# Fewer weight chunks ahead of the first unit, decoded one unit later, and GpSimd's adds in reverse order

## The chip, the cores and the metric

The kernel runs on one core of one Trainium2 chip. The metric is the device time of one execution in microseconds (us); the time before the change is the median of three runs, 1470.31 us. Engines are called as in the profile: PE is TensorE's matmul and PEld its weight load, DVE is VectorE, ACT is ScalarE, POOL is GpSimd, SP is SyncE. ACTq and SPq are the sequencers that issue DMAs for ScalarE and SyncE.

## The reference

Attention with a top-32 mask, then a feed-forward block with the gate h * cos(h), on 8 batches of 8 heads, 576 positions, 64 values a head:

```
scores = q @ k.T / sqrt(64)                      # per batch and head
kth    = 32nd largest score of each row
attn   = softmax(where(scores >= kth, scores, -1e9))
x      = concat over heads (attn @ v)            # 4608 x 512
h      = x @ w_in                                # w_in: 512 x 2048
out    = (h * cos(h)) @ w_out                    # w_out: 2048 x 512
```

q, k and v are float32. The two weight matrices are float64: the kernel reads the two 32-bit words of every value and decodes them to float32 itself.

## The kernel before, in words

**Units and slots.** The work is cut into units: 128 tokens times one pair of heads (NP = 4 pairs), 144 units in all. A loop of slots runs over them. In slot i, VectorE searches the 32 largest scores of unit i in four rounds (L361 MAX8 and L366 MATCH_REPLACE8), on two folded halves of each row: `rest` holds the larger ones (made by VectorE, L256) and `low` the smaller ones (made by GpSimd, L274 and L283; in units 7 to 10 by VectorE, L264). In the same slot ScalarE masks and exponentiates the scores of unit i-1 (L390, L392, L400) and copies the scores of unit i+1 out of PSUM (L241, L244); GpSimd splits the exponentials of unit i-2 into 16-bit halves (L433, L435), which SyncE writes to DRAM (L443) and reads back transposed (L449); TensorE computes scores of later units (L229) and, every other slot, the values of two older units (L486), which VectorE takes over into `xT` (L495).

**Feed-forward.** As soon as the four units of a block of 128 tokens are done, TensorE also does the feed-forward matmuls of that block (L546 with w_in, L621 with w_out); ScalarE takes the first ones out of PSUM (L560, L562) and computes the sine (L601), GpSimd reduces and gates (L582, L591, L608).

**Weights.** The weights come in 32 chunks of 512 KB, 16 of w_in (numbers 0 to 15) and 16 of w_out. Each chunk goes through four steps, each with its own queue in `wq`:

- `load_weights`: the DMA into a staging tile `st` (L123). There are 7 tiles of tag "g", which the feed-forward shares later, and 4 of tag "x", which odd chunks below number 12 take.
- `decode_first`: two ScalarE operations (L136, L139) on the two words.
- `decode_second`: a shift on VectorE (L147, TENSOR_SCALAR).
- `decode_third`: an add on GpSimd (L157, TENSOR_TENSOR), after which the chunk is done.

In a slot, `load_weights` stands at the start, `decode_second` and `decode_third` between the third and the fourth round of the search, and `decode_first` at the end. So a chunk loaded in slot i is shifted and added in slot i+1. Ahead of slot 0 the kernel loads chunks 0 and 1 over SyncE's queue and six more over ScalarE's, and runs `decode_first` on four of them.

**What sets the order.** The order of instructions on each engine is the order of the program: an engine works its queue from front to back, and the DMAs that ScalarE issues stand in the same queue as its computing instructions. TensorE's feed-forward work is drawn slot by slot by a credit, and only from chunks that were done when the slot began:

```
wq["ready"] = wq["done"]
```

DMAs signal completion on eight semaphores, shared by both queues. A DMA is issued only when the DMA that had the same semaphore before it has landed.

Of the kernel before, what the change touches and what calls it, by code (L numbers as in the profile page):

```python
# [30 lines left out]
def kernel(  # L31
# [16 lines left out]
    NP = H // 2  # L48
# [37 lines left out]
    for i in range(DF // CW):  # L86
        w = consts.tile([P, NC, CW], F32, tag=f"w_in{i}", name=f"w_in{i}")
# [4 lines left out]
    for f in range(NF):  # L92
        w = consts.tile([P, DM], F32, tag=f"w_out{f}", name=f"w_out{f}")
# [6 lines left out]
    wq = {"next": 0, "loaded": deque(), "second": deque(), "third": deque(), "done": 0, "ready": 0}  # L100

    def staged(spare=0):
        return sum(c[2] == spare for k in ("loaded", "second", "third") for c in wq[k])

    def load_weights(n, queue=None):
        queue = queue or nc.scalar
        for _ in range(n):
            i = wq["next"]
            if i >= len(chunks):
                return  # L110
            src, dst = chunks[i]
            if not DECODE:
                queue.dma_start(out=dst, in_=src)
                wq["next"] = wq["done"] = i + 1
                continue
            spare = i < 3 * XB and i % 2 == 1 and staged(1) < XB
            if spare:
                st = ffw.tile([P, CW, 2], I32, tag="x", name="st", bufs=XB)
            elif staged() + ff["live"] >= CHUNKS:
                return  # L120
            else:
                st = ffw.tile([P, CW, 2], I32, tag="g", name="st", bufs=CHUNKS)
            queue.dma_start(out=st.rearrange("p w i -> p (w i)"), in_=src)  # L123
            wq["loaded"].append((st, dst, int(spare)))
            wq["next"] = i + 1
# [4 lines left out]
    def decode_first(n):  # L130


        for _ in range(min(n, len(wq["loaded"]))):
            st, w, spare = wq["loaded"].popleft()
            lo, hi = st[:, :, 0], st[:, :, 1]
            nc.scalar.activation(  # L136
                out=w, in_=hi.bitcast(F32), func=AF.Prelu, scale=2.0**-111, alpha=2.0**32
            )
            nc.scalar.mul(out=lo, in_=lo.bitcast(U32), mul=2.0**-29)  # L139
            wq["second"].append((st, w, spare))  # L140

    def decode_second(n):

        for _ in range(min(n, len(wq["second"]))):
            st, w, spare = wq["second"].popleft()
            wi = w.bitcast(I32)
            nc.vector.tensor_scalar(  # L147
                out=wi, in0=wi, scalar1=3, scalar2=None, op0=ALU.logical_shift_left
            )
            wq["third"].append((st, w, spare))  # L150

    def decode_third():

        while wq["third"]:
            st, w, _ = wq["third"].popleft()
            wi = w.bitcast(I32)
            nc.gpsimd.tensor_tensor(out=wi, in0=wi, in1=st[:, :, 0], op=ALU.add)  # L157
            wq["done"] += 1
# [63 lines left out]
    def scores(u):  # L222
        sc = u["sc"] = ps.tile([P, 2, 512], F32, tag="sc", name="sc", bufs=2)
        for to, k0, k1 in ((sc, 0, SB), (sc_ends[u["n"] % 2], SB, S)):
            for b, q0, rows, r0 in u["parts"]:
                for j in range(2):
                    d = slice(j * D, (j + 1) * D)
                    st = pairs[b, u["hp"]]
                    nc.tensor.matmul(  # L229
                        to[r0 : r0 + rows, j, 0 : k1 - k0],  # L230
                        st["q"][d, q0 : q0 + rows],
                        st["k"][d, k0:k1],
                        start=True,
                        stop=True,
                    )
# [42 lines left out]
    def fold_low(u):  # L278

        if not u["folds"] or u["n"] in BUSY:  # L280
            return
        low = u["low"].bitcast(I32)
        nc.gpsimd.tensor_tensor(  # L283
            out=low, in0=low, in1=u["rest"][:, :, HS:S].bitcast(I32), op=ALU.subtract
        )
# [15 lines left out]
    def topk_first(u, w):  # L301

        u["top"] = tops[u["n"] % len(tops)]
        merges = w and w["folds"]
        if merges:
            merge_first(w)
        if u["folds"]:
            if u["n"] not in BUSY:
                fold_sum(u)
            fold_high(u)  # L310
        else:
            u["rest"] = work.tile([P, 2, S], F32, tag="rest", name="rest", bufs=1)
        if merges:
            merge_second(w)
        if u["folds"] and u["n"] in BUSY:
            fold_now(u)
        topk_round(u, 0, [lambda: bounds(w), lambda: distances(w)] if w else ())

    def topk_round(u, rnd, between=(), ahead=None):
        top, rest, lasts = u["top"], u["rest"], TOPK // 8 - 1  # L320
        end = TOPK - 1 - 8 * rnd
        at = top[:, :, end : end - 8 if rnd < lasts else None : -1, 0]
        if u["folds"]:
            search(
                at, rest[:, :, HS:S] if rnd == 0 else rest[:, :, 0:HS], rest[:, :, 0:HS], rnd < lasts,
                between if rnd < lasts else (),
            )
        else:
            search(at, u["s"] if rnd == 0 else rest, rest, rnd < lasts, between)
        if rnd < lasts:  # L330
            return
        del u["rest"]
        if u["folds"]:
            low = u.pop("low")
            for k in range(TOPK // 16):
                more = k < TOPK // 16 - 1
                if ahead and not more:
                    take_values(ahead)
                search(
                    top[:, :, 1 + 8 * k : 9 + 8 * k, 1], low, low, more,  # L340
                    () if more or rnd < lasts else between,
                )
# [225 lines left out]
    def take_banks():  # L568
        while full:
            take, *what = full.popleft()  # L570
            take(*what)
# [83 lines left out]
    def feed(n):  # L655

        ff["tick"] += 1
        while n > 0 and ff["credit"] >= 1:
            for kind in (ff["kind"], 1 - ff["kind"]):
                if (can_first, can_second)[kind]():  # L660
                    break
            else:
                return
            if kind == 0:
                ff1(*first.popleft())
            else:
                ff2(*second.popleft())
            if kind != ff["kind"] or ff["half"]:
                ff["kind"], ff["half"] = 1 - kind, 0
            else:  # L670
                ff["half"] = 1
            n, ff["credit"] = n - 1, ff["credit"] - 1
# [24 lines left out]
    for n in range(NP, len(order)):  # L697
        i = last[order[n - 5]] if n >= 5 else 0
        load_at(max(i, 2 * NP + 2), load_qk, *order[n])
        i = last_values[order[n - 6]] if n >= 6 else 0  # L700
# [13 lines left out]
    def send(x):  # L714

        split(x)
        write_halves(x)
        transposes(x)

    def slot(i, u, w, x, z):  # L720
        n = 0 if i == 0 else 4 if i == 1 else 3 if i < NP else 2
        if i < NP:
            for load, b, hp in at_once[i]:
                load(b, hp)
        load_weights(n)
        if x:
            send(x)
        topk_first(u, w)
        fold_low(u)
        topk_round(u, 1)  # L730
        topk_round(u, 2)
        decode_second(NP)
        decode_third()
        made = scored.get(i, [])
        if z:
            take_banks()
        feed(1)

        for m in made:
            scores(m)  # L740
        if z:
            values(z)


        late = len(made) > 0

        decoding = i < 3 * NP
        if i % 2 or decoding:
            sines(1)
        if w:  # L750
            mask(w)
        take_banks()
        if w and late:
            exponentials(w)
        take_scores(units[i + 1])
        if w and not late:
            exponentials(w)
        topk_round(u, 3, both(w), z)
        if i in at_slot:
            load, b, hp = at_slot[i]  # L760
            load(b, hp)
        gate(1)
        feed(1 if len(made) == 2 else 2)
        take_banks()
        decode_first(NP)
        reduce_first()
        reduce_second()
        feed(1 if len(made) == 2 else 3)
        if i == LAST:
            sines(1)  # L770
# [46 lines left out]
    load_weights(2, nc.sync)  # L817
    scores(units[0])
    take_scores(units[0])
    load_weights(2 * NP - 2)  # L820
    decode_first(NP)
    for i in range(NU + 1):
        ff["end"] = i >= NU
        ff["credit"] = min(ff["credit"] + 5.0 - 0.9 * len(scored.get(i, [])), 5.3)
# [2 lines left out]
        u, w = (units[i - n] if 0 <= i - n < NU else None for n in range(2))  # L827
# [53 lines left out]
```

## Time and profile before

| | us |
|---|---|
| runs | 1470.68, 1468.21, 1470.31; median 1470.31 |
| profiled execution, its own time | 1467.61 |
| its span, first to last instruction | 1465.8 |
| busy PE | 1387.1 (95%) |
| busy DVE | 1363.0 (93%) |
| busy POOL | 1162.2 (79%) |
| busy ACT | 1086.8 (74%) |
| granted TensorE clock, mean | 0.972 |

The span is that of the profiled execution; 1.8 us of its own time lie outside it. A row of the timeline reads: start, duration, engine, line of the kernel, operation, output<-input, shape, count, and in brackets the idle time before it and what ended that wait. "x4" with one duration means four instructions in a row, from the first one's start to the last one's end. Times are from the start of the span.

### The profile page before, as it was taken

The page shows a single profiled execution, that of the slowest core. Times are in us where ns is not written, and L with a number is a line of the kernel's source. Part 1 is how long each engine was busy: PE and PEld are TensorE (multiplying, and loading weights), DVE is VectorE, ACT ScalarE, POOL GpSimd, SP SyncE. Part 2 cuts the span into 40 slices and gives each one's busy share as a digit, 9 for nine tenths or more (in the row PEclk, how much of TensorE's full clock was granted, in tenths as well). Part 3 has the DMA queues.
Part 4 walks back from the last instruction along what each step waited for, and adds up shares of the span by engine and source line. Part 5 has one row for each costly group of instructions (what it writes and reads, how often), then busy time and mean ns, then how long its engine had stood idle before and what let it go on. Part 6 is the DMA issues. An engine that isn't in the chain of part 4 may idle for free.

```text
span 1465.8 us, 30264 instructions
## 1 busy us (share of the span) xinstructions
PE 1387.1 (95%) x10290; PEld 996.1 (68%) x10290; DVE 1363.0 (93%) x5213; ACT 1086.8 (74%) x1911; POOL 1162.2 (79%) x814
## 2 busy tenths in 40 slices
PE   3378899999999999999999999999999999999998
PEld 2165667777777767777777767777777777777765
DVE  5999999999999999999999999999999999999831
ACT  5677777777777777777777777777777787777651
POOL 4978888888888887888888888888888888888510
PEclk6589999999999999999999999999999999999999
DMA  8777686666665566657665666656666466755200
GB/s 264 241 227 189 179 197 176 158 159 182 179 167 152 147 189 182 167 143 186 189 166 146 152 171 187 176 147 172 190 166 162 138 172 175 168 151 143 70 8 15
DMA packets 427433, 239.99 MB, mean 164 GB/s; under 512 B 375952, under 2 KB 392592, under 8 KB 427280
## 3 DMA queue, kind: packets, MB, share of 16 engines
q1 hardware_dynamic: 417552, 212.69, 55.2%
q10 hardware_dynamic: 9728, 25.38, 5.0%
q8 instruction: 81, 1.33, 0.4%
q14 instruction: 72, 0.59, 0.1%
HBM read 45.09 MB, written 101.19 MB: 100 GB/s over the span
## 4 chain that ended last, share of the span: by engine, by line
PE 81%; DVE 13%; ACT 4%; DMA 2%; issue 0%; POOL 0%; SPq 0%; ACTq 0%; POOLq 0%
PE mm L546 31%; PE o L621 31%; PE rim L486 10%; PE sc L229 7%; DVE top L361 6%; DVE rest L366 3%; PE rim L229 2%; DVE rest L256 1%; DVE low L366 1%; ACT s L400 1%; DMA st<-in_moe_w_in_dram 1%; DMA k<-in_k_dram 1%; DVE w_in L147 1%; ACT s L392 1%; ACT L400 1%
## 5 line engine op out<-in xcount | busy, mean ns | idle before, releaser
L546 PEld LDWEIGHTS mm<-xT,w_in 128*128 128x128 f32 x4608 | 536.6, 192 | 70.6 <-issue 64.1
L621 PE MATMUL o<-w_out,g 128*128 128x512 f32 x1152 | 538.9, 601 | 9.9 <-POOL g L608 8.7
L546 PE MATMUL mm<-xT,w_in 128*128 128x128 f32 x4608 | 539.9, 275 | 3.9 <-ACT x L562 2.0
L361 DVE MAX8 top<-rest 128x8 f32<-128x288 f32 x1148 | 480.6, 453 | 0.0
L433 POOL COPY halves<-s 128x2304 uint16<-128x2304 uint16 x140 | 294.4, 2103 | 151.2 <-ACT s L400 149.6
L366 DVE MATCH_REPLACE8 rest<-top,rest 128x288 f32<-128x288 f32 (+1 forms) x860 | 376.8, 445 | 0.0
L621 PEld LDWEIGHTS o<-w_out,g 128*128 128x128 f32 x1152 | 203.4, 191 | 199.4 <-issue 187.1
L361 DVE MAX8 top<-low 128x8 f32<-128x288 f32 x568 | 239.7, 447 | 0.0
L400 ACT ACTIVATE s<-s,nd 128x576 f32<-128x576 f32 x288 | 220.1, 767 | 1.2 <-ACT ob L631 0.4
L392 ACT ACTIVATE s<-s,top 128x576 f32<-128x576 f32 x288 | 206.2, 766 | 0.0
L283 POOL TENSOR_TENSOR low<-low,rest 128x576 int32<-128x576 int32 x138 | 194.8, 1411 | 10.8
L274 POOL TENSOR_TENSOR low<-s 128x576 int32<-128x576 int32 x138 | 194.6, 1410 | 6.9 <-ACT s L246 4.8
L229 PE MATMUL sc<-k,q 64*128 64x448 f32 (+1 forms) x640 | 157.2, 591 | 42.4 <-DVE rest L256 24.4
L560 ACT ACTIVATE g<-mm 128x512 f32<-128x512 f32 x144 | 85.8, 596 | 130.2 <-PE mm L546 126.0
L591 POOL TENSOR_TENSOR x<-g,x 128x1024 f32<-128x1024 f32 x68 | 160.8, 2365 | 5.7
L608 POOL TENSOR_TENSOR g<-g,x 128x1024 f32<-128x1024 f32 x68 | 160.8, 2364 | 1.6 <-ACT x L601 1.6
L486 PE MATMUL rim<-pT,v 128*64 128x128 f32 (+1 forms) x2560 | 159.0, 268 | 0.0
L486 PEld LDWEIGHTS rim<-pT,v 128*64 128x64 f32 x2560 | 132.5, 139 | 10.0 <-issue 2.0
L241 ACT COPY s<-sc 128x896 f32<-128x896 f32 x143 | 128.2, 897 | 0.5 <-PE sc L229 0.5
L366 DVE MATCH_REPLACE8 low<-top,low 128x288 f32<-128x288 f32 x284 | 123.5, 442 | 0.0
L244 ACT COPY s<-rim 128x256 f32<-128x256 f32 x144 | 55.0, 382 | 90.6 <-PE rim L486 90.6
L229 PEld LDWEIGHTS sc<-k,q 64*128 64x128 f32 (+1 forms) x640 | 46.7, 182 | 105.5 <-DVE rest L366 47.2
(62 smaller groups left out, 1336.4 us busy)
## 6 DMA issues: line engine op xcount, KB each, us to landing
rows<-halves SPq DMA_DIRECT2D x140, 640.0 KB, 3.0
out_dram<-ob ACTq DMA_DIRECT2D x36, 256.0 KB, 2.2
q<-in_q_dram SPq DMA_DIRECT2D x31, 288.0 KB, 3.8
v<-in_v_dram SPq DMA_DIRECT2D x32, 256.0 KB, 3.2
st<-in_moe_w_out_dram ACTq DMA_DIRECT2D x16, 512.0 KB, 5.4
st<-in_moe_w_in_dram ACTq DMA_DIRECT2D x14, 512.0 KB, 6.0
k<-in_k_dram SPq DMA_DIRECT2D x31, 144.0 KB, 3.7
k<-in_k_dram SPq DMA_DIRECT2D x32, 128.0 KB, 3.7
```

The costliest lines, as they stand in the source:

```text
L229: nc.tensor.matmul(to[r0 : r0 + rows, j, 0 : k1 - k0], st["q"][d, q0 : q0 + rows], st["k"][d, k0:k1], start=True, stop=True,)
L274: nc.gpsimd.tensor_tensor(out=u["low"].bitcast(I32), in0=s[:, :, 0:HS], in1=s[:, :, HS:S], op=ALU.add)
L283: nc.gpsimd.tensor_tensor(out=low, in0=low, in1=u["rest"][:, :, HS:S].bitcast(I32), op=ALU.subtract)
L361: nc.vector.max(to[:, j], src[:, j])
L366: nc.vector.match_replace(rest[:, j], to[:, j], src[:, j], NEG)
L392: nc.scalar.activation(out=s[:, j], in_=s[:, j], func=AF.Prelu, bias=less[:, j, 1:2], scale=1.0, alpha=FAR)
L400: nc.scalar.activation(out=s[:, j], in_=s[:, j], func=AF.Exp, bias=nd[:, j : j + 1], scale=SCALE, accum_out=den[:, j, 0:1],)
L433: nc.gpsimd.tensor_copy(out=halves[:, :, 0 : 2 * S], in_=s.rearrange("p (k h) -> p h k", h=2))
L486: nc.tensor.matmul(o[d, to], lhsT, rhs, start=c == 0, stop=c == NT)
L546: nc.tensor.matmul(mm[:, at : at + w], w_in[f // FC][:, c, (f % FC) * P : (f % FC + 1) * P], blk["xT"][:, c], start=c == 0, stop=c == NC - 1,)
L591: nc.gpsimd.tensor_tensor(out=x, in0=g, in1=x, op=ALU.subtract)
L621: nc.tensor.matmul(o, g[:, at : at + P], w_out[f], start=f == 0, stop=f == NF - 1)
```

## The change

Three edits. In the prologue, two weight chunks are issued on ScalarE's queue in place of six, and no `decode_first` runs there; the first chunks are decoded at the end of slot 0 and are shifted and added in slot 1. In `slot`, three chunks are loaded in slots 2 to 7 instead of in slots 2 and 3 only. In `decode_third`, the chunks of a slot are added from the last shifted one to the first.

```
     def decode_third():
 
         while wq["third"]:
-            st, w, _ = wq["third"].popleft()
+            st, w, _ = wq["third"].pop()
...
     def slot(i, u, w, x, z):
-        n = 0 if i == 0 else 4 if i == 1 else 3 if i < NP else 2
+        n = 0 if i == 0 else 4 if i == 1 else 3 if i < 2 * NP else 2
...
     load_weights(2, nc.sync)
     scores(units[0])
     take_scores(units[0])
-    load_weights(2 * NP - 2)
-    decode_first(NP)
+    load_weights(2)
```

The number of chunks that are shifted and added in each slot:

| slot | 0 | 1 | 2 | 3 | 4 | 5 | 6 | 7 | 8 | 9 | 10 | 11 |
|---|---|---|---|---|---|---|---|---|---|---|---|---|
| before | 4 | 4 | 4 | 3 | 3 | 2 | 2 | 2 | 2 | 2 | 2 | 2 |
| after | 0 | 4 | 4 | 3 | 3 | 3 | 3 | 3 | 3 | 2 | 2 | 2 |

The sequence of TensorE's instructions is the same in both kernels.

## The prediction

> **What bounds the kernel now.** I read the page's 40 slices first, then a table of windows, then the chain of waits, then the timeline of the first 60 us. In the slices each digit is tenths busy:
>
> ```profile
> PE   3378899999999999999999999999999999999998
> DVE  5999999999999999999999999999999999999831
> ```
>
> ```profile
> 0.00:207.00 207.00, 137.98 (x926) 95.67 (x926) 187.72 (x702) 144.38 (x267) 157.35 (x126) 0.80 0.77 218
> 560.00:850.00 290.00, 290.00 (x2214) 210.96 (x2214) 286.06 (x1116) 226.35 (x398) 248.91 (x171) 1.00 0.62 164
> ```
>
> The columns are window, length, busy PE, PEld, DVE, ACT, POOL. From about 207 us TensorE has no gap (290.00 of 290). Before that it misses 69 us, and the chain is VectorE's: from 24 us to 108 us it is nothing but DVE rows, and PE takes it over at 207.43. The change leaves TensorE's sequence of instructions as it is, so it can only move the moment at which that full stretch starts; what VectorE gains or loses by slot 10 (124 us) moves the end by as much. VectorE has one large hole, in slot 0:
>
> ```profile
> 12.41 0.44 DVE L366 MATCH_REPLACE8 rest<-top,rest 128x288 f32<-128x288 f32 x1
> ...
> 20.02 0.43 DVE L147 TENSOR_SCALAR w_in<-w_in 128x512 int32<-128x512 int32 x1 [7.17 <-ACT w_in L136]
> 21.13 1.53 DVE L147 TENSOR_SCALAR w_in<-w_in 128x512 int32<-128x512 int32 x2 [0.68 <-ACT w_in L136]
> 23.34 0.75 DVE L147 TENSOR_SCALAR w_in<-w_in 128x512 int32<-128x512 int32 x1 [0.69 <-ACT w_in L136]
> 24.02 0.81 DVE L361 MAX8 top<-rest 128x8 f32<-128x288 f32 x2
> ```
>
> From 12.85 to 24.02 VectorE does four shifts and otherwise waits for ScalarE. ScalarE stands in its own queue:
>
> ```profile
> 6.79 12.50 ACTq L123 DMA_DIRECT2D st<-in_moe_w_in_dram  x5
> ...
> 19.33 0.66 ACT L136 ACTIVATE w_in<-st 128x512 f32<-128x512 f32 x1 [12.12 <-DMA v_tail<-in_v_dram]
> ```
>
> The last five of its six weight loads take 12.50 us to issue, because each first waits for the earlier DMA on the same completion semaphore (the program has eight), and the decode follows them in order. A second, smaller loss is in slot 2:
>
> ```profile
> 43.08 1.41 POOL L283 TENSOR_TENSOR low<-low,rest 128x576 int32<-128x576 int32 x1
> 43.27 4.71 DVE L147 TENSOR_SCALAR w_in<-w_in 128x512 int32<-128x512 int32 x4
> 44.91 5.45 POOL L157 TENSOR_TENSOR w_in<-w_in,st 128x512 int32<-128x512 int32 x4 [0.41 <-DVE w_in L147]
> ...
> 56.88 1.09 DVE L147 TENSOR_SCALAR w_in<-w_in 128x512 int32<-128x512 int32 x3
> ```
>
> Four shifts cost 4.71 us beside GpSimd's work (three of about 1.51, one of 0.41), three cost 1.09 where GpSimd was idle.
>
> **What the Trainium skill says.** "SBUF — State Buffer", section "Who interferes with whom": VectorE and GpSimd share a port pair under an exclusive lock, tensor_scalar on VectorE can take it, and whichever starts first blocks the other for the whole instruction. The trace agrees: shifts blocked at 43.27; at 33.49 the reverse, an add of 2.02 instead of 1.3 us beside a batch of shifts. "DMA: Bandwidth & Descriptors", section "Issuing engines are not separate DMA queues": loads of ScalarE and SyncE run on the same engines and interleave. It agrees: from 12 to 24 us the DMA share is 1.03 at 305 GB/s, with both queues loading.
>
> **The parts.** D_i is the start of slot i on VectorE (its L349; slot 0 starts at 7.24 with L256).
>
> (1) Slot 0 without decode. Removed: four L147, their waits, and from ScalarE's queue four loads ahead of slot 0 (and four L136/L139 pairs ahead of the copies of unit 1). VectorE: 7.24 to 12.85, then the rest of the slot (24.02 to 27.15 = 3.1), so D_1 = 15.95 instead of 27.15: **-11.2 us**. Cover needed: unit 1's scores, done by 9.3, whose copies (L241, L244: 1.3) now follow the two loads issued by about 7.2 and end at 10.6; GpSimd's low, done at 10.18.
>
> (2) Where the decode of chunks 0 to 3 goes. On ScalarE it now follows those copies. Chunks landed at 9.99, 11.2, 14.3 and 16.6 (moments at which SyncE's waiting DMAs went); with nothing of chunks 4 to 7 in the way I take 15.3 for the fourth. L136+L139 cost 1.12 a chunk: done at 16.5, long before slot 1's shifts (D_1+5.8 = 21.7). Costs VectorE nothing there; the batch of four stands where another four stood.
>
> (3) Chunks 4 to 7 are now issued by ScalarE in slot 1, behind that decode and ahead of unit 0's L390, L392, L400 and unit 2's copies. On SyncE's queue nothing is moved, but v of pair 0 now waits for chunk 0 where it waited for chunk 1 (1.2 earlier). ScalarE's last load waits by its semaphore for v of pair 1, which SyncE issues after q and k of pair 3, these after chunk 3. By bytes: chunks 0-3, four q/k pairs and two v are 5.05 MB, with chunks 4-6 up to 6.6; at 0.305 MB/us from about 2 us on, 18.5 to 24; I take 21.3. Then mask 1.7, exponentials 1.6, copies 1.3: unit 2 is ready at 25.9, for a D_2 of 15.95 + 10.33 = 26.3. Covered by 0.4; a stall of 0 to 2.3, I take 0.3, most of which GpSimd's delay in (4) would cost anyway. Slots 2 and 3 have 2 to 3 us of slack: there ScalarE waited 7.58 us at 54.42 and VectorE lost nothing.
>
> (4) GpSimd's order and the lock. Its slot is L433, L435, L274, L283 = 5.28 (50.30 to 55.58), then the adds, 1.22 each once the shifts are over (34.36 to 39.25 for four). In reverse order the first add waits for the last shift, so shifts no longer alternate with adds. By itself that costs nothing where the lock held the first add anyway, and no matmul waits for it: `wq["ready"]` counts only chunks of earlier slots. A batch that meets L274 or L283 loses between 0 and 1.4. Slot 2: adds of slot 1 end at 23.0+4.9 = 27.95, L283 at 33.25; shifts wanted at 32.1 wait for it, then run three at 0.34: end 34.55, D_3 = 37.65 (slot 11.4, before 13.6: -2.2). Slot 3: adds end 39.45, L283 44.75, shifts wanted at 43.4: 1.3 lost. Slot 4: L283 54.7 against 54.6: 0.3. From slot 5 on none, with 0.3 to spare.
>
> (5) Three chunks instead of two in slots 5 to 8: a third shift, 0.34 each in 5 to 7, **+1.0**. In slot 8 the third shift and add (0.34+1.22) delay GpSimd's L608 and L591, which TensorE (4.36 us at 113.44) and ScalarE's sine (1.01 at 116.87) already wait for; VectorE then waits 1.9 for ScalarE: **+1.6**. The third pair on ScalarE in slot 7 (1.12), where it is busy 11.95 of 12 us, runs in parallel with that. Bounds of this step: 0.34 if all of it hides, 2.7 if both add. DMA: the same 32 loads.
>
> Sum, with each slot's start (before / estimate):
>
> | D_1 | D_2 | D_3 | D_4 | D_5 | D_6 | D_7 | D_8 |
> |---|---|---|---|---|---|---|---|
> | 27.15 | 37.48 | 51.10 | 61.09 | 71.48 | 81.14 | 91.20 | 101.49 |
> | 15.95 | 26.3 | 37.7 | 48.8 | 59.2 | 69.2 | 79.6 | 90.2 |
>
> Gain 11.3 at D_8, less 1.6 in slots 8 and 9, less 0.4 for (3) and unseen waits: **9.3**. From slot 9 on both kernels decode two chunks a slot, and all after it shifts. Profiled execution: 1467.61 (span 1465.8 and 1.8 around it), so 1458.3; the median of the runs is 2.7 above it, so 1470.3 - 9.3 = **1461.0**.
>
> **Rivals.** A: nothing is given back: no collisions from slot 2 on, slot 8's extra add hidden. For: margins are tenths of a us. Against: the waits at 113.44 and 116.87. Gain 13.4 less 0.34 four times = 12, plus 1 if slot 2 is clean: 1457.3 to 1458.3. B: GpSimd becomes the bound. With three adds and no overlap its slot is 5.28+3.66+1.05 = 10.0, as long as VectorE's 9.99; a shift that waits a whole L283 (up to 1.4) in slots 3 to 7 gives 5 back: gain 3 to 5, 1465.3 to 1467.3. C, slower: ScalarE's load issue blocks every slot. Before, in slot 3, it stood until a transposing DMA had landed; VectorE had about 2 us of slack. If in slots 1 to 8 each issue comes over 3.5 us later against VectorE than before, 8 slots lose over 1.5 each, 12.2 in all, and the gain turns into 2.9 lost: 1473 to 1476. Against: one such wait was seen, and fewer loads are outstanding. D: the hole only moves: unit 2's copies wait for v of pair 1 until 32 instead of 21.3; it decides nothing below 21.7, and equals the forecast's whole gain above 32. Against: that needs half the DMA rate seen. About 1470.
>
> **Numbers.** Forecast 0.58, A 0.15, B 0.17, C 0.05, D 0.05. 0.2% of the time, 2.9 us, is about what a measurement can tell from no change. Faster: forecast, A and most of B, 0.86; same: D and some of B, 0.08; slower: C and a little of D, 0.06. The range takes A whole and B to its end: 1457.0 to 1467.3.
>
> **What would show it.** Right: L361 follows L366 at 12.8 without idle; slot 1's L349 near 16, slot 2's near 26; no L147 batch of four at 4.7; TensorE's full stretch from about 198. Wrong: idle of VectorE before slot 2's L256 or at L408 of slots 1 to 3 (step 3), L147 at 1.5 in slots 3 to 7 (step 4), an equal gap at slot 9 (step 5), or gaps of TensorE after 200 us.

## The result, and the profile after

The kernel after takes 1476.33 us (median of 4 runs, 1475.66 to 1476.9) beside 1469.26 us for the kernel before in the same comparison: ratio 1.0049, interval [1.0032, 1.0067]. It is **7 us slower** where 9.3 us of gain were predicted. The profiled execution took 1476.9 us, 9.3 more than that of before; its span is 1474.9 us, 9.1 more. A later series of 22 runs of the same kernel gave 1475.27 us, ratio 1.0036 [1.0023, 1.0049], 6 us slower.

The same slices of the page as were shown of before, and the row of the DMA engines:

```profile
PE   4367899999999999999999999999999999999999
DVE  7988999999999999999999999999999999999831
DMA  8897577557675576756765666666665556755300
```

VectorE's first slice has filled, from 5 tenths to 7: the hole of slot 0 is gone. But its third and fourth slices now stand at 8 where they stood at 9, and the table of windows (length, busy PE, PEld, DVE, ACT, POOL, PE clock, DMA share, GB/s) shows fewer instructions done in the first 207 us, not more:

```profile
0.00:207.00 207.00, 134.61 (x880) 94.39 (x881) 179.08 (x667) 138.41 (x255) 148.34 (x121) 0.78 0.78 210
560.00:850.00 290.00, 290.00 (x2170) 210.42 (x2171) 285.86 (x1115) 227.41 (x394) 247.02 (x169) 1.00 0.62 166
```

VectorE is at 667 instructions where it was at 702. TensorE has again no gap later on, so the start decides here too, only with the other sign. The timeline of VectorE in slots 0 to 2:

```profile
12.88 0.44 DVE L366 MATCH_REPLACE8 rest<-top,rest 128x288 f32<-128x288 f32 x1
13.24 0.81 DVE L361 MAX8 top<-rest 128x8 f32<-128x288 f32 x2
...
28.32 0.16 DVE L408 TENSOR_REDUCE den<-dens 128x2 f32<-128x4 f32 x1 [2.07 <-ACT s L400]
28.40 0.45 DVE L361 MAX8 top<-low 128x8 f32<-128x288 f32 x1
29.38 0.76 DVE L256 TENSOR_TENSOR rest<-sc,s 128x576 f32<-128x576 f32 x1 [0.27 <-ACT s L244]
35.04 1.42 DVE L147 TENSOR_SCALAR w_in<-w_in 128x512 int32<-128x512 int32 x4
```

L361 follows L366 at 13.24 with no wait; the four shifts of slot 2 take 1.42 us where they took 4.71. That is what the change was to do. In slot 1 VectorE now waits 2.34 us for ScalarE (2.07 at L408 and 0.27 at L256), because ScalarE stands in its queue for three loads until 25.2. The start of each slot on VectorE, in us and against before:

| slot | before | after | difference | slot | before | after | difference |
|---|---|---|---|---|---|---|---|
| 1 | 27.15 | 16.38 | -10.77 | 7 | 91.20 | 93.10 | **+1.90** |
| 2 | 37.48 | 28.89 | -8.59 | 8 | 101.49 | 103.72 | +2.23 |
| 3 | 51.10 | 39.58 | -11.52 | 9 | 112.59 | 117.16 | +4.57 |
| 4 | 61.09 | 52.16 | -8.93 | 10 | 124.03 | 131.10 | +7.07 |
| 5 | 71.48 | 63.29 | -8.19 | 11 | 134.72 | 143.86 | +9.14 |
| 6 | 81.14 | 73.28 | -7.86 | 19 | 214.35 | 222.37 | +8.02 |

Up to slot 6 the gain stands at 7.86. Slot 6 alone takes 19.82 us where it took 10.06 and gives back 9.76; slots 7 to 10 lose 7.24 more. The timeline of slot 6 (a row of SPq is SyncE issuing a DMA, its duration the time until it was issued):

```profile
63.45 4.17 SPq L449 DMA_TRANSPOSE pT<-rows  x1
...
67.72 0.53 SPq L443 DMA_DIRECT2D rows<-halves  x1
...
77.82 6.87 SPq L449 DMA_TRANSPOSE pT<-rows  x1
77.88 2.10 POOL L433 COPY halves<-s 128x2304 uint16<-128x2304 uint16 x1 [3.81 <-DMA rows<-halves]
...
79.07 3.27 DVE L147 TENSOR_SCALAR w_out<-w_out 128x512 int32<-128x512 int32 x3
83.62 0.82 DVE L361 MAX8 top<-low 128x8 f32<-128x288 f32 x2 [0.56 <-POOL low L283]
...
91.78 0.49 DVE L495 TENSOR_TENSOR xT<-rim,pT 128x128 f32<-128x128 f32 x2 [6.49 <-ACT s L244]
```

And the chain of waits through it (start, length, what):

```profile
77.82 10.98 DMA pT<-rows
88.80 0.14 issue
88.94 2.42 PE rim L486 x20
91.38 0.38 ACT s L244
91.78 0.49 DVE xT L495 x2
```

It is read backwards. VectorE waits 6.49 us at L495, for ScalarE's copy L244, for TensorE's values L486, for the transposing DMA, which took 10.98 us from the start of its issue to its landing. It reads what the row write of 67.72 (unit 3) wrote, so it could not be issued before that had landed: 10.1 us lie between the two. In the kernel before, the row write of the same unit and its transposing DMA stand here:

```profile
74.23 0.53 SPq L443 DMA_DIRECT2D rows<-halves  x1
...
78.16 4.42 SPq L449 DMA_TRANSPOSE pT<-rows  x1
```

There the second follows the first after 3.9 us and lands after 6.5. A smaller part of the delay is SyncE's own queue: in the kernel after, GpSimd had unit 3's halves ready at 66.0, but the row write stood until 67.72 behind the transposing DMA of the unit before, whose issue took 4.17 us. The late row write also holds `halves`, so GpSimd's split starts 3.81 us late and its work meets VectorE's three shifts, which take 3.27 instead of 1.09. The view of DMA issues between 60 and 96 us, kernel before, gives from issue to landing (last column, us):

```profile
st<-in_moe_w_out_dram ACTq DMA_DIRECT2D x8, 512.0 KB, 5.6
rows<-halves SPq DMA_DIRECT2D x4, 640.0 KB, 4.5
pT<-rows SPq DMA_TRANSPOSE x4, 6.8
```

The kernel after in the same window:

```profile
st<-in_moe_w_out_dram ACTq DMA_DIRECT2D x9, 512.0 KB, 6.3
rows<-halves SPq DMA_DIRECT2D x3, 640.0 KB, 8.6
pT<-rows SPq DMA_TRANSPOSE x3, 11.0
```

Three loads a slot instead of two are 9 against 8 in this window, because slot 6 became longer. The medians are of few DMAs and hide how unlike these are. Singly, the three loads of slot 5, issued between 63.33 and 64.78, took 4.2, 8.8 and 11.7 us, the transposing DMA of 63.45, whose issue was done at 67.62, took 12.8, and unit 3's row write after it 10.0. The five landed in the order in which their issue was done, so the third load was as late as the DMAs behind it; but it is for these that TensorE waits. In a second profile of the same kernel (`after_again`, below) the medians are 5.6, 8.2 and 7.6 us: the row writes are slow again, the transposing DMAs less so.

### The profile page after: what moved, and what is told of

It is laid out like the page before. It is cut to its first block, busy times and chain, and to the rows that moved or that the text cites. A ratio compares the mean times of both kernels' runs of the same rounds, so it can differ in the third digit from the quotient of the medians.

```text
span 1474.9 us, 30236 instructions
## 1 busy us (share of the span) xinstructions
PE 1393.1 (94%) x10290; PEld 1000.3 (68%) x10290; DVE 1363.6 (92%) x5213; ACT 1087.5 (74%) x1911; POOL 1161.2 (79%) x814
## 4 chain that ended last, share of the span: by engine, by line
PE 82%; DVE 9%; ACT 4%; DMA 4%; POOL 1%; issue 1%; SPq 0%; ACTq 0%; POOLq 0%
PE o L621 31%; PE mm L546 31%; PE rim L486 11%; PE sc L229 8%; DVE top L361 4%; DVE rest L366 3%; PE rim L229 2%; DMA pT<-rows 1%; DMA st<-in_moe_w_in_dram 1%; ACT s L400 1%; DVE rest L256 1%; ACT s L392 1%; DMA k<-in_k_dram 1%; DMA v<-in_v_dram 0%; DVE low L366 0%
## 5 line engine op out<-in xcount | busy, mean ns | idle before, releaser
L621 PE MATMUL o<-w_out,g 128*128 128x512 f32 x1152 | 540.3, 603 | 9.2 <-POOL g L608 8.0
L361 DVE MAX8 top<-rest 128x8 f32<-128x288 f32 x1148 | 480.8, 454 | 0.0
L366 DVE MATCH_REPLACE8 rest<-top,rest 128x288 f32<-128x288 f32 (+1 forms) x860 | 377.1, 446 | 0.0
L621 PEld LDWEIGHTS o<-w_out,g 128*128 128x128 f32 x1152 | 203.9, 191 | 198.9 <-issue 187.7
L361 DVE MAX8 top<-low 128x8 f32<-128x288 f32 x568 | 240.1, 448 | 1.1 <-POOL low L283 1.1
L229 PE MATMUL sc<-k,q 64*128 64x448 f32 (+1 forms) x640 | 158.6, 588 | 28.8 <-DVE rest L256 11.0
L486 PE MATMUL rim<-pT,v 128*64 128x128 f32 (+1 forms) x2560 | 160.0, 269 | 17.7 <-DMA pT<-rows 15.3
L486 PEld LDWEIGHTS rim<-pT,v 128*64 128x64 f32 x2560 | 133.0, 139 | 28.1 <-issue 12.3
L244 ACT COPY s<-rim 128x256 f32<-128x256 f32 x144 | 54.9, 381 | 100.7 <-PE rim L486 100.7
L366 DVE MATCH_REPLACE8 low<-top,low 128x288 f32<-128x288 f32 x284 | 123.6, 443 | 0.0
L256 DVE TENSOR_TENSOR rest<-sc,s 128x576 f32<-128x576 f32 x142 | 106.2, 748 | 6.9 <-ACT s L246 6.6
```

Of the source, the lines that this page charges most:

```text
L229: nc.tensor.matmul(to[r0 : r0 + rows, j, 0 : k1 - k0], st["q"][d, q0 : q0 + rows], st["k"][d, k0:k1], start=True, stop=True,)
L361: nc.vector.max(to[:, j], src[:, j])
L366: nc.vector.match_replace(rest[:, j], to[:, j], src[:, j], NEG)
L486: nc.tensor.matmul(o[d, to], lhsT, rhs, start=c == 0, stop=c == NT)
L621: nc.tensor.matmul(o, g[:, at : at + P], w_out[f], start=f == 0, stop=f == NF - 1)
```

## The experiments

### Is it the bytes of the third load?

**`a_noload`**, the kernel after with the third load of slots 5, 6 and 7 left out:

```
+            if i in (19, 22, 25):
+                wq["loaded"].append((wq["last"], dst, 0))
+                wq["next"] = i + 1
+                continue
...
+            wq["last"] = st
```

> The kernel after, with the third weight load of slots 5, 6 and 7 (chunks 19, 22 and 25) left out; the shift, add and ScalarE operations of these chunks stay at full size and work on the staging tile of the chunk before, so the values of three weight chunks are not those of the reference. Theory 1 (DMA): three loads a slot hold up the DMAs that write and transpose the exponentials; unit 3's transposed block lands late and VectorE waits 6.5 us at L495 of slot 6. Then this wait falls below 1.5 us, slot 7 starts near 85 to 87 us instead of 93.1, and the time is 1464 to 1469. Theory 2 (engines): the third decode a slot, on ScalarE, VectorE and GpSimd, with its waits for the shared port, is what costs; then all of that is still there, and the time stays within 2 us of the kernel after (1474 to 1478).

Measured: 1466.75 us, ratio to before 0.9983 [0.9972, 0.9994]. Slot 7 starts 4.26 us ahead of before, where after was 1.90 behind. So the time is that of theory 1, but not all of the loss is gone in this execution: L495 of slot 6 still waits 2.12 us, slot 6 loses 3.85 us where after lost 9.76, and at slot 11 nothing is left of the gain (0.14 behind before).

**`b_copy`**, the kernel before with a DMA of 512 KB from DRAM to DRAM on ScalarE's queue in slots 5, 6 and 7, which nobody reads:

```
+        if i in (5, 6, 7):
+            copy = dram.tile([P, 2 * CW], I32, tag="copy", name="copy", bufs=3)
+            nc.scalar.dma_start(out=copy, in_=chunks[i][0])
```

> The kernel before, with one more DMA of a weight chunk's size (512 KB, DRAM to DRAM, nobody reads it) issued by ScalarE after the loads of slots 5, 6 and 7; no decode is added. Theory 1 (DMA): slots 6 and 8 get a wait at L495, and the time rises by 4 to 10 us, to 1473 to 1479. Theory 2 (engines): no engine has more to do, the time stays within 2 us of 1469.

Measured: 1470.62 us, ratio 1.0012 [1.0001, 1.0022]. All slots up to 6 start within 0.18 us of before; slot 7 starts 3.48 late. The timeline of that kernel has the wait at the same line:

```profile
90.52 1.98 PE L486 MATMUL rim<-pT,v 128*64 128x128 f32 x16 [3.62 <-DMA pT<-rows]
...
93.37 0.49 DVE L495 TENSOR_TENSOR xT<-rim,pT 128x128 f32<-128x128 f32 x2 [3.12 <-ACT s L244]
```

Bytes alone, without a decode, make the same wait in the same slot, as theory 1 said. The time is that of theory 2: 0.1% more, and the span of the profiled execution is 0.2 us longer than that of before, although slot 11 still starts 3.47 late. The wait is smaller than 9.8; in this kernel the row writes took 5.8 and the transposing DMAs 8.8 us between 60 and 96 us, between those of before and of after. That VectorE, 8 us later here, leaves them more slack is argued and not shown; the copy also writes DRAM where a load writes SBUF.

**`a_tiny`** separates the bytes from what else a load brings, its place in ScalarE's queue and its completion semaphore. As `a_noload`, but a load of 8 KB is issued in the place of each one left out:

```
+            if i in (19, 22, 25):
+                few = ffw.tile([P, 16], I32, tag="few", name="few", bufs=3)
+                queue.dma_start(out=few, in_=src[:, 0:16])
+                wq["loaded"].append((wq["last"], dst, 0))
...
```

> The kernel after, in which the third load of slots 5, 6 and 7 (chunks 19, 22, 25) carries 8 KB into a tile of its own in place of 512 KB; the decode of these chunks stays and works on the previous staging tile. So the place in ScalarE's queue and the completion semaphores are as after, and only the bytes are gone. T1 (bytes on the shared DMA engines hold the row write and the transposing DMA): as with the loads left out, slot 7 starts 3 to 8 us before that of before, median 1464 to 1469. T2 (the third load's wait for a semaphore, in ScalarE's queue ahead of exponentials and copies, is what costs): slot 6 loses 8 us or more as after does, slot 7 starts about 2 us late, median 1473 to 1478.

Measured: 1467.21 us, ratio 0.9973 [0.9958, 0.9987]. Slot 6 takes 10.50 us, slot 7 starts 7.81 ahead of before. Its DMA issues between 60 and 96 us:

```profile
rows<-halves SPq DMA_DIRECT2D x3, 640.0 KB, 4.7
pT<-rows SPq DMA_TRANSPOSE x4, 5.9
few<-in_moe_w_out_dram ACTq DMA_DIRECT2D x3, 8.0 KB, 5.4
```

The second theory falls: the third load keeps its place in the queue and its semaphore, and holds that for 5.4 us, about as long as a weight load does, but the row write is back at 4.7 us, the transposing DMA at 5.9, and slot 6 loses 0.44 us. For unit 3 alone the row write takes 5.4 us (after: 10.0) and the transposing DMA 6.8 (11.0). `a_tiny` still issues the third load and decodes the third chunk; what it lacks is 3 x 0.5 MB.

How much half a megabyte costs differs between executions. Unit 3's row write took 10.0, 11.6, 9.9 and 14.3 us in the four profiles that have the third load (this kernel, `after_again`, `a_popleft` and `popleft_again`, below), 7.9 in `a_noload` and 5.4 in `a_tiny`. At the 224 to 301 GB/s that the kernel after and `a_tiny` moved from 64 to 68 us, the bytes themselves are worth about 2 us, an estimate. What makes the rest no run shows.

### The order of GpSimd's adds

**`a_popleft`** is the kernel after with this order undone, as below; **`b_pop`** is the kernel before with the reverse order alone, the same edit the other way round:

```
-            st, w, _ = wq["third"].pop()
+            st, w, _ = wq["third"].popleft()
```

> The kernel after, with GpSimd's adds back in the order of the shifts. Theory 1 (DMA): the order has little part in the loss; slot 2 gets its L147 batch of about 4.7 us back unless GpSimd's timing has moved away from it, and the time is 1475 to 1479. Theory 2 (engines, the adds starting later in particular): the time falls by 3 us or more, to 1473 or less.

> The kernel before, with only GpSimd's adds reversed. If the first add's wait for the last shift keeps shifts and adds apart, the batch of slot 2 falls from 4.71 us to about 2.6 and everything after it comes 2 us earlier, unless a later wait absorbs it: 1467 to 1469.5. If the reversal costs (adds later, so low and the split later), 1470 to 1472.

Measured: `a_popleft` 1470.87 us, ratio 1.0018 [0.9998, 1.0038], 12 runs from 1463.08 to 1479.33: the figure of theory 2, the order has a part in the loss. `b_pop` 1473.2 us, ratio 1.002 [1.0004, 1.0036], so there the reversal costs as well, while its profiled execution is the quickest of its 12: 1466.63, under the 1467.61 of before. Slot by slot that execution does what step 4 says. The four shifts of slot 2 and three of slot 3, `b_pop`:

```profile
42.97 1.42 DVE L147 TENSOR_SCALAR w_in<-w_in 128x512 int32<-128x512 int32 x4
53.97 2.58 DVE L147 TENSOR_SCALAR w_in<-w_in 128x512 int32<-128x512 int32 x3
```

Slot 2 is 2.61 us shorter than before (step 4, worked out for the kernel after: 2.2), slot 3 is 1.49 longer (1.3) and slot 4 0.14 longer (0.3).

The 16 us between the runs of `a_popleft` asked for more runs, of it and of the kernel after side by side, unchanged, under new names:

> The kernel after, unchanged, in more runs. T1 (the loss of slot 6 is the same in every execution): median 1474 to 1478, slot 6 again near 20 us, slot 7 starting 0 to 4 us late. T2 (the size of the collision varies from execution to execution, as the 16 us spread of the version with the order of adds undone suggests): runs from about 1465 to 1479, median 1469 to 1473.

> The kernel after with the order of GpSimd's adds as before, in more runs. T1 (the reverse order costs 5 us in the kernel after): 1469 to 1472, and at least 3 us under the kernel after beside it. T2 (the 5 us were spread between executions): within 2 us of the kernel after beside it.

Measured: after 1475.27 us, 22 runs from 1468.46 to 1484.32; with the order undone 1471.47 us, 22 runs from 1462.93 to 1477.15, ratio to before 1.0008 [0.9994, 1.0023]; before in the same series 1469.21 us, 43 runs from 1466.63 to 1472.98. So two things are true. The kernel after is 3.8 us slower with the reverse order, more than half of its 6 us against before, with intervals that just touch (1.0023). And both kernels with three loads in slots 5 to 7 spread over 14 to 16 us where before spreads over 6 (8 to 13 in three other series). The loss of slot 6 itself is in all four profiles of the pair: it takes 19.82 and 18.46 us with the reverse order, 16.41 and 19.04 without. (In `after_again` VectorE waits 4.44 us for GpSimd's `low` and 3.43 at L495, both behind unit 3's row write, which took 11.6 us there.) What differs is how slots 7 to 10 go on (7.24, 2.34, 2.84 and 8.15 lost), and that has no order in it. Where the 3.8 us arise these profiles don't show.

### The rest: slots 8 to 10

**`a_noload6`** is `a_noload` with all loads from chunk 17 on left out (`if i >= 17`), **`a_noload6s`** leaves out the third chunk's shift and add of slot 8 as well:

```
+            wq["n2"] = wq.get("n2", 0) + 1
+            if wq["n2"] == 26:
+                wq["done"] += 1
+                continue
             nc.vector.tensor_scalar(
```

> The kernel after, with every weight load from chunk 17 on left out (slots 5 to 11); their ScalarE, VectorE and GpSimd operations stay and work on the staging tile of the last loaded chunk, so these weight chunks are not those of the reference. Theory 1 (DMA): what is lost after slot 6 in the kernel after is lost to transposed blocks that land late beside weight loads. Then no wait for them is left in slots 6 to 10, and of the 7.9 us gained at the start of slot 6 only the engines' part is given back (three shifts, 1.0, and GpSimd's third add in slot 8, 1.6): slot 11 starts 4 to 6 us earlier than before, time 1463 to 1466. Theory 2 (engines): the gain is given back anyway in slots 8 to 10, where GpSimd's add holds up the gate and so TensorE; slot 11 starts within 1.5 us of before, time 1468 to 1471.

> The kernel after with all loads from chunk 17 on left out (their decode stays, on the previous staging tile), and in slot 8 the third chunk's shift and add left out as well. With those loads out but the shift and add in place, slot 8 takes 14.15 us on VectorE (before 11.10): L613 (before's L608) starts 11.56 us into the slot where it started 9.53 into it before, and TensorE waits 6.47 for it. T1 (the third shift and add in slot 8 push that gate back, as step 5 of the prediction says, and TensorE pays more than the push): L613 about 2 us earlier, slot 8 at most 12.2, slot 9 starts at least 6.2 us before that of before. T2 (TensorE's own work sets slot 8, whatever GpSimd does): slot 8 stays above 13.5.

Measured: `a_noload6` 1466.01 us, ratio 0.9967 [0.9957, 0.9978]; `a_noload6s` 1467.81 us, ratio 0.9977 [0.9966, 0.9989]. In `a_noload6` slot 7 starts 7.60 ahead of before and slot 11 only 2.44, between what the two theories gave: without any load from slot 5 on, slots 7 to 10 still lose 5.2. Taking the shift and add out of slot 8 did not tell why. GpSimd's gate came 9.95 us into the slot instead of 11.56, and TensorE waited 3.54 for it instead of 6.47, but the slot lasted 14.10 us as before (14.15). The timeline of VectorE in `a_noload6s`:

```profile
109.99 0.49 DVE L504 TENSOR_TENSOR xT<-rim,pT 128x128 f32<-128x128 f32 x2 [3.19 <-ACT s L253]
```

ScalarE was the late one. Its copy L253 ended at 109.95, behind decodes that had waited 1.40 for GpSimd: the chunks left out share one staging tile, so ScalarE's write into it waits for GpSimd's add. That wait is the experiment's own, `a_noload6` has the like of it (1.38 us in slot 8), and the result of both for these slots is **inconclusive**. Of the runs here `a_tiny`, where only three chunks share a tile with the one before, tells most of the loss of slots 8 to 10 without the extra bytes: it loses 1.17, 0.82 and 1.67, 3.7 in all.

### Moving the bytes elsewhere

If the bytes are the matter, fewer in slots 5 to 7 should keep the gain. Three versions load four chunks in each of the first slots and two from then on. **`a_early`** does it in slots 1 to 3, **`a_early4x`** in slots 1 to 4 with the staging tiles of tag "x" open to odd chunks below 20, **`a_early4sx`** does the latter on SyncE's queue. The edit of the last one (`a_early` has only the first pair of lines, with `i < NP`; `a_early4x` the first two):

```
-        n = 0 if i == 0 else 4 if i == 1 else 3 if i < 2 * NP else 2
+        n = 0 if i == 0 else 4 if i <= NP else 2
...
-            spare = i < 3 * XB and i % 2 == 1 and staged(1) < XB
+            spare = i < 5 * XB and i % 2 == 1 and staged(1) < XB
...
-        load_weights(n)
+        load_weights(n, nc.sync if i <= NP else None)
```

> The kernel after, with four loads in slots 1 to 3 and two from slot 4 on, as before from slot 4 on. Theory 1 (DMA): the loads now lie where no transposed block is waited for soon; the gain of slot 0 (8 us at slot 6 in the kernel after) survives, L495 of slot 6 waits under 1 us, and the time is 1459 to 1465. Theory 2 (engines): the decode work moves forward into slots 2 to 4, where GpSimd is as full; a third to two thirds of the loss remains, 1468 to 1474.

> The kernel after, with four loads in slots 1 to 4 and two from slot 5 on (the four spare staging tiles serve up to chunk 19), so that from slot 4 on as many chunks are done as before and TensorE's sequence is that of before. Theory 1 (DMA): loads in slots 5 to 7 are as few as before, so L495 of slots 6, 8 and 10 waits under 1 us and slot 11 starts 4 to 7 us earlier than before; 1463 to 1466. Theory 2 (engines): the extra adds and shifts lie in slots 2 to 5; GpSimd's low comes late there, and the gain at slot 6 is under 4 us, time 1466 to 1470.

> As a_early4x, and the loads of slots 1 to 4 are issued by SyncE (after its q, k and v loads) instead of ScalarE. If ScalarE's blocked queue is what cost 2.3 us in slot 1, 3.4 in slot 2 of a_early and 1.8 in slot 3 of the kernel after, these waits (L408 for L400) vanish: slot 2 starts at 26 to 27 us, slot 6 8 to 12 us earlier than before; time 1458 to 1463. If the data itself lands too late (the rate is what limits), the waits only change their name to L147 or L136 and the time is that of a_early4x.

| | median us | ratio to before | slot 2 | slot 4 | slot 7 | slot 11 | slot 20 |
|---|---|---|---|---|---|---|---|
| after (first series) | 1476.33 | 1.0049 [1.0032, 1.0067] | -8.59 | -8.93 | +1.90 | +9.14 | +8.02 |
| `a_early` | 1469.12 | 0.9993 [0.998, 1.0006] | -8.77 | -7.77 | -5.26 | -4.98 | -0.31 |
| `a_early4x` | 1466.33 | 0.9974 [0.9962, 0.9986] | -8.40 | -7.10 | +0.45 | +0.72 | +0.17 |
| `a_early4sx` | 1464.93 | 0.9968 [0.9957, 0.9979] | -10.76 | -11.52 | -5.08 | -3.28 | -4.11 |

(Slots: start against before, one profiled execution each.) In all three slot 6 loses at most 1.6 us of the 9.8; `a_early` waits 0.15 us at L495 there. What they lose, they lose elsewhere. In `a_early4x` VectorE waits 2.98 and 2.94 us at L408 in slots 1 and 2, for exponentials behind four loads in ScalarE's queue, and slot 4, which now has four loads, takes over the wait at L495, 3.82 us. `a_early4sx` has those loads on SyncE and none of these waits: slot 2 starts at 26.72, within half a microsecond of the 26.3 of the prediction. It gives back 3.88 us in slot 5, where its four shifts take 4.64 us beside GpSimd. `a_early` keeps its 5 us up to slot 12 and then waits 2.05, 1.70 and 2.72 us for GpSimd's `low` in slots 12 to 14. `a_early4sx` beats both kernels, by 4.7 us the one before, but not the 1458 to 1463 that were expected of it; its interval and that of `a_early4x` overlap, so the queue shows in the starts of the slots and not surely in the time. `a_early` has the wait of theory 1 and the time of theory 2, and `a_early4x` comes close to the time of theory 1 with nothing gained at slot 11.

**`a_early4sxq`** is that version with the order of the adds undone (`popleft`):

> The version with four loads in each of slots 1 to 4 on SyncE's queue (1464.9 before), and in it the order of GpSimd's adds as before. T1 (the reverse order is worth what step 4 says: a batch of four shifts at 4.7 instead of 1.4 us comes back in slots 2 to 4, and no other place changes): 2 to 4 us slower, 1466 to 1469. T2 (the reverse order costs several us further on, as undoing it in the kernel after seemed to say): 1459 to 1463.

Measured: 1465.36 us, ratio 0.9963 [0.9952, 0.9974]: the same as with the reverse order, within the intervals. The long batches are back in its timeline (slots 2, 4 and 5):

```profile
31.56 4.69 DVE L147 TENSOR_SCALAR w_in<-w_in 128x512 int32<-128x512 int32 x4
...
55.48 5.73 DVE L147 TENSOR_SCALAR w_in<-w_in 128x512 int32<-128x512 int32 x4
70.51 5.01 DVE L147 TENSOR_SCALAR w_out<-w_out 128x512 int32<-128x512 int32 x4
```

and slot 7 starts 2.50 ahead of before instead of 5.08, but it keeps all of the 2.50 to slot 11. Both theories were off: neither the 2 to 4 us that the batches should cost nor a gain showed in the time.

## Why the prediction was wrong

The prediction had slot 11 start 9.7 us ahead of before; in the profiled execution it starts 9.1 behind. Of these 18.8 us, 4.1 arise before slot 6 (step 3), 9.4 in slot 6 (step 5, its words on DMA) and 5.3 in slots 8 to 10 (step 5, the rest). Over many runs step 4 has a part in it too.

**(1) Slot 0 without decode: right.** -11.2 predicted, -10.77 measured. VectorE starts at 7.71 instead of 7.24; the search runs through without a gap.

**(2) Decode on ScalarE: right in its effect, nothing waits for it in slot 1.** The four shifts of slot 1 stand where they were expected.

**(3) Chunks 4 to 7 on ScalarE in slot 1: right kind, mis-sized.** 0 to 2.3 us were given and 0.3 taken; it is 2.07 at L408 plus 0.27 at L256. The timeline of ScalarE says why:

```profile
17.77 7.43 ACTq L123 DMA_DIRECT2D st<-in_moe_w_in_dram  x3
25.24 0.20 ACT L390 ACTIVATE nd<-nd 128x2 f32<-128x2 f32 x1 [7.90 <-DVE top L361]
```

The last load is issued at 25.2, not at 21.3 as worked out by bytes. That `a_early4sx`, with these loads on SyncE, starts slot 2 2.2 us earlier than after shows the price of the place in the queue. The step also took slots 2 and 3 to have 2 to 3 us of slack. In slot 3 of the kernel after ScalarE's L390 comes behind two loads that are issued at 45.59 and after, and VectorE waits 1.82 us at L408; `a_early4sx` has no such wait. With these, 7.86 us of gain reach slot 6 where 11.9 were forecast.

**(4) Order and lock: right to some tenths in the slots shown, wrong in "By itself that costs nothing".** `b_pop` shows the former. Over many runs the reverse order went with 3.8 us in the kernel after, 0.2% in before and nothing in `a_early4sx`. The step puts this at nothing; where and why it arises stays open, since the one profile of `b_pop` is of its quickest execution.

**(5) Three chunks in slots 5 to 8: this step failed**, in its last sentence, "DMA: the same 32 loads". Its engine part was good: slots 5 and 7 are 0.33 us longer each, as forecast. But three loads a slot instead of two put the row write at 8.6 us and the transposing DMA at 11.0, and slot 6 lost 9.76 us. The total of loads is the same; their neighbours are not. In slot 0 the deferred loads had run ahead of the first row write (41.66 in the kernel before), at a DMA share of 1.03; the prediction had read this share and had concluded nothing about where these bytes would go. In slots 5 to 7 the row write and the transposing DMA share the 16 engines, and TensorE, ScalarE and VectorE wait for them in a chain. The section of the Trainium skill that the prediction cited, "DMA: Bandwidth & Descriptors", section "Issuing engines are not separate DMA queues", says that the DMAs of different queues run on the same engines and interleave; `a_tiny` shows that in slot 6 this, and not the queue they stand in, sets the price. A likely other half of the miss is that with VectorE 8 us ahead the slack that had hidden the transposed blocks is used up: the bytes alone cost 3.3 us in slot 6 (`b_copy`), being ahead without them 0.44 (`a_tiny`) or 3.85 (`a_noload`), both together 9.76. No run shows this by itself, since the bytes of `b_copy` are a copy within DRAM.

The rest of step 5, +1.6 in slots 8 and 9, is near the 2.0 us that these lose in `a_tiny`, without the bytes; in the kernel after they lose 4.8. Slot 10, for which the step has no term, loses 1.7 and 2.1. How this splits between the third decode and DMAs stays open, since `a_noload6s` brought a wait of its own.

**The rivals.** C gave 1473 to 1476 and the right sign, but in the main by another mechanism, so this was luck: it had ScalarE's load issue late in eight slots. That happened in slots 1 and 3 (2.34 and 1.82 us). The loads of slots 5 and 6 were issued in 0.33 to 1.83 us, and `a_tiny` keeps those issues without the loss. B (GpSimd as the bound) and D (the hole only moves) did not come about: 7.86 us of gain were there at slot 6. The case that came true, one late row write and its transposing DMA worth the whole gain, was not among the rivals.

**The sum.** For the profiled execution: 7.86 gained by slot 6, 9.76 lost in it, 7.24 lost in slots 7 to 10, 1.1 won back by slot 19, and the span ends 9.1 late. That the end moves as slot 11 does, on which the prediction rests, holds here; in other profiles it is off by some us (`b_copy`: 3.47 late at slot 11, 0.2 at the end).

## What to carry to other kernels

When loads are deferred, cost the bytes where they go, not only the engines' work: list which DMAs with a waiting consumer run in those slots, and what slack each has once the gain has moved the engines forward. A hole of an engine may be a time in which the DMA engines are full; filling it hands their work to a later stage. If the loads must move, the version that took them early and on a queue without computing instructions (here SyncE's, slots 1 to 4) kept 4 to 5 us of the 11. A time that spreads over 16 us from run to run needs more than four runs: the first four of the kernel after lay within 1.3 us.

## What the runs showed of the hardware that was not expected

**One more 512 KB load delays the DMAs behind it, and a median hides it.** With three loads in slot 5, unit 3's 640 KB row write took 9.9 to 14.3 us in four profiles, without the third 5.4 and 7.9 in two, and in the kernel before 3.8. The median of the loads (6.3 against 5.6 us) hardly moved, while the third load of slot 5 took 11.7 us.

**A wait of TensorE can cost twice.** In the kernel after, the eight L621 of slot 10 take 6.07 us; in the kernel before the same eight take 3.70. The row of after, and the windows around it (the clock is the third column from the end):

```profile
131.54 6.07 PE L621 MATMUL o<-w_out,g 128*128 128x512 f32 x8 [5.42 <-POOL g L608]
```

```profile
128.00:130.00 2.00, 0.00 (x0) 0.00 (x0) 1.09 (x4) 1.99 (x4) 2.00 (x2) 0.88 0.65 234
130.00:132.00 2.00, 0.46 (x1) 0.46 (x2) 1.46 (x7) 2.00 (x5) 2.00 (x2) 0.50 0.92 274
...
136.00:138.00 2.00, 2.00 (x6) 0.80 (x6) 2.00 (x9) 0.68 (x2) 0.00 (x0) 0.91 1.09 387
```

After 5.42 us of waiting the granted clock is 0.50 and comes back at about 136 us, so the wait is paid again in slower matmuls: 2.4 us more. In before the wait ahead of them was 1.74 us and the clock stayed at 1.00; a wait of 4.36 us there (at 113.44) is followed by 0.50 too. The Trainium skill, "TensorE: Matmul & The Clock Gate", section "Part 1: The HAM clock gate (the "warmup" mystery)", states that the clock falls to half after an idle window of about 3.4 us and returns after as long a busy one. These rows agree on the fall: the wait began at 126.1, and 0.88 from 128 to 130 puts the fall near 129.5, 3.4 us later. The return came 4.8 us after the matmuls had begun again. A step that prices a wait of TensorE of this length has to add this.

**The clock column can be wrong.** In the profile of `a_tiny` it stands at 1.00 from 60 to 95 us, but four L229 (there L236) matmuls at 73.92 take 1.86 us, as the same four do in the kernel after at a clock of 0.50 (74.32); at 94.68 four of them take 1.02. Here the durations decide.
